# Three weight pieces issued ahead of the last batch's load in the Fourier stage, with a new order table

## The chip, the cores and the metric

The kernel runs on one core of one Trainium2 chip, as one launch. The metric is the time of a launch on the device in microseconds (us). Before the change three runs took 1112.25, 1106.89 and 1110.59 us; their median is 1110.59 us. The profiled execution, from which every duration below comes, is a fourth one: it took 1107.66 us, of which its span (first to last instruction) is 1105.9 us.

## The reference

Three blocks follow one another on inputs of batch 4, sequence 576 and width 512 (8 heads of 64):

```python
# 1. attention with a relative-position bias from a small MLP
scores = q @ k.T / 8 + bias                     # bias: relu(x * w1 + b1) @ w2, per head
x = softmax(scores) @ v                         # 4 x 8 x 576 x 64 -> x: 4 x 576 x 512
# 2. Fourier mixing, layer norm, MLP
u = x + real(fft(fft(x, axis=1), axis=2))
un = (u - mean(u)) / sqrt(var(u) + 1e-6)
x = u + relu(un @ w_ch1) @ w_ch2                # 512 -> 2048 -> 512
# 3. spatial gating
h = relu(x @ w_in)                              # 512 -> 1024, halves u and v
v_s = w_spatial @ normalize(v) + b_spatial
out = (u * v_s) @ w_out
```

## The kernel before, in words

The kernel is a sequence of phases on one core: the bias, attention, the Fourier stage, the MLP and the gating. Matrix products are done in float32 on TensorE (PE); VectorE (DVE), ScalarE (ACT) and GpSimd (POOL) prepare and evict; all loads and stores of these phases stand in one queue, SyncE's (SP).

**Attention.** A loop over `d` takes two units of 128 rows per step, 72 steps and eight more to drain (`attention_phase`). Every second pair of probability tiles is transposed by a DMA (`turn`, L483); PE reads it three steps later (`back`, L519). Finished rows go to a buffer in device memory, `xd[b]`, one per batch (`store`, L569 and L572). At the end of each step the loop calls `after(n)`, with `n = d - 72`.

**Loads for the Fourier stage.** `after` is made by `first_folds`. A batch's load (`Folds.loads`, L747) reads `xd[b]` back in six parts: 128, 128, 127, 128, 1 and 64 rows of 512 numbers (256, 256, 254, 256, 2 and 128 KB), after a step that only writes zeros. For batch 0 the steps are spread over attention: one is taken at `n = -36, -34, ...` until they are used up. Batches 1 and 2 are loaded at `n = 0` and `n = 3`. Batch 3 needs the last rows that attention stores, and is loaded in the Fourier stage.

**Fourier stage.** Per batch `b`: DVE folds the rows (`T0`, `X0`, `F00`, `F01`, then `T1`, `X1`, `F10`, `F11`; L764, L775, L782); PE makes four products `pe`, `me`, `po`, `mo` with the cosine and sine tables (L877), each into one of two PSUM banks `y`; ACT copies each out (`keep`, L881) and so frees the bank; PE makes `D` from two of them (`second`, L907, one PSUM tile for all), ACT evicts it (`d`, L914), PE transposes the rows into one of two tiles `xs` (`residual`, L895 and L897), and DVE adds the two, twice per half: `+` (L917) and `-` (L925), which frees `xs`. ACT also copies corners (L884), gathers (L888) and one crossed row (`r`, L922).

**What else runs in that stage** (`early`): the MLP's first four weight pieces and its first normalisation. A piece `w0` to `w3` (`piece`) is a DMA of 512 KB from SP into one of three staging buffers `w64` (L1695); ACT scales it (`wsq`, L1034), DVE merges it with three instructions (L1041, L1044, L1047), which frees the buffer, and ACT and DVE split it (L1703, L1706). The sums, means and squares of the first chunks (L1616 to L1677) are `n0`, `n1`, `h`, `l`, `q`, `a`, `f0`, `n2`, `c1`.

**What sets the order.** `Plan.run` builds one list out of all these operations, each with assumed durations, resources to take and give, and what it comes after. It repeatedly emits the operation with the smallest start time less its `RANK`. Each engine then executes its own operations strictly in that order: one that waits holds up all behind it on its engine. SP likewise: a DMA whose issue waits holds up all issues behind it. After the stage the MLP's first product is L1358 (`h`), whose weight pieces go on through `Weights.step` (L1072).

Of the kernel before, what the change touches and what calls it, by code (L numbers as in the profile page):

```python
# [18 lines left out]
B, H, S, D = 4, 8, 576, 64  # L19
# [624 lines left out]
def phases(tc, nc, io, vs, low, raw, xd, ident, tables, after, right):  # L644
# [28 lines left out]
W_SCALE = 2.0**-112  # L673
TP = 290
T2 = 289
F_LOAD = -36
X_LOAD = 0, 3
FOLDS = {2: 2, 3: 2, 4: 2, 5: 2}
YB = 2
AFTER = (0,)  # L680
PRINT = False
RANK = {
# [4 lines left out]
}  # L687
READY = 0.0, 2.0, 6.0, 14.0

# [103 lines left out]
def first_folds(folds):  # L793

    todo, loads = [], folds.loads(0)

    def after(n):
        if F_LOAD <= n < 0 and n % 2 == 0:
            next(loads, int)()
        if n == 0:  # L800
            folds.open()
            todo.extend(folds.steps(0))
        if n in X_LOAD:
            folds.load(1 + X_LOAD.index(n))
        for _ in range(FOLDS.get(n, 0)):
            todo.pop(0)[2]()

    return after
# [45 lines left out]
def fft_phase(tc, nc, folds, tabs, ut, bank, extra, es):  # L854
# [14 lines left out]
    def stage1(b, nm):  # L869
        F = folds.two[b % 2]  # L870
        y = ps[b, nm] = ps_y.tile([128, 512], F32, tag="y", name="y")
        z, o = dict(pe=(0, 0), me=(0, 129), po=(1, 0), mo=(1, 128))[nm]
        seq = [(128, F[z][0:r, k, o : o + 128], tt[0:r, z, k]) for k, r in rows]
        if nm == "po":
            seq[1:1] = [(1, F[0][0:r, k, 128:129], tt[0:r, 0, k]) for k, r in rows]
        for n, (m, st, mv) in enumerate(seq):
            nc.tensor.matmul(out=y[0:m, 0:TP], lhsT=st, rhs=mv, start=(n == 0), stop=(n == len(seq) - 1))  # L877

    def keep(b, nm):
        ys[b, nm] = yp.tile([128, TP], F32, tag=nm, name="y", bufs=YB)  # L880
        nc.scalar.activation(out=ys[b, nm], in_=ps.pop((b, nm))[:, 0:TP], func=AF.Copy)  # L881

    def corner(b):
        nc.scalar.activation(out=xs[b][:, :, 0:1], in_=xs[b][:, :, 256:257], func=AF.Copy)  # L884

    def gather(b, e, s):
        col = 257 + e if s else e
        nc.scalar.activation(out=folds.near[e][:, :, s], in_=xs[b][:, :, col : col + 255 : 2], func=AF.Copy)  # L888

    def residual(b, e, y):  # L890

        t = Xs[b, e, y] = ps_x.tile([128, 2, 512], F32, tag="xs", name="xs")
        for s in range(2):
            for k in (0, 1):
                nc.tensor.transpose(t[:, s, 128 * k : 128 * k + 128], folds.near[e][:, 3 * y + k, s], ident)  # L895
            i = ident[0:65, 64::-1] if y else ident[0:65, 0:65]
            nc.tensor.transpose(t[:, s, 256:321], folds.near[e][0:65, 2, s], i)  # L897

    def second(b, e):
        D = Ds[b, e] = ps_d.tile([128, 2, 512], F32, tag="D", name="D")  # L900
        for s in range(2):
            if e == 0:
                seq = [(fs[:, s], ys[b, "pe"]), (fs[:, 2 + s], ys[b, "po"])]
            else:
                seq = [(fs[:, 4], ys[b, "me"]), (fs[:, 5 + s], ys[b, "mo"])]
            for n, (st, mv) in enumerate(seq):
                nc.tensor.matmul(out=D[:, s, 0:TP], lhsT=st, rhs=mv, start=(n == 0), stop=(n == len(seq) - 1))  # L907
# [4 lines left out]
    def evict(b, e):  # L912
        d = ds[b, e] = yp.tile([128, 2, TP], F32, tag="d", name="d", bufs=2)
        ends[1] = nc.scalar.activation(out=d, in_=Ds[b, e][:, :, 0:TP], func=AF.Copy)  # L914

    def add(b, e):
        nc.vector.tensor_tensor(  # L917
            out=out(b, e)[:, :, 0:T2], in0=Xs.pop((b, e, 0))[:, :, 0:T2], in1=ds[b, e][:, :, 0:T2], op=ALU.add
        )

    def cross(b):
        nc.scalar.activation(out=ds[b, 0][0:1], in_=Ds[b, 0][0:1, ::-1, 0:TP], func=AF.Copy)  # L922

    def mirror(b, e):
        ends[0] = nc.vector.tensor_tensor(  # L925
            out=out(b, e)[:, :, T2:S], in0=Xs.pop((b, e, 1))[:, :, 287:0:-1], in1=ds.pop((b, e))[:, ::-1, 287:0:-1],
            op=ALU.add,
        )

    plan = Plan({"y": 2, "xs": 2, "D": 1, "d": 2, "F0": 1, "F1": 1, "n0": 1, "n1": 1, "w64": 3, "wsq": WSQB})  # L930
    add_op = plan.add
    for b in range(B):
        f = f"F{b % 2}"
        if b == B - 1:
            add_op("load", "load", [("SP", 0.5)], lambda: folds.load(B - 1), start=3.0)
        if b:
            last = (b - 1, "F11") if b > 1 else None
            for nm, us, go in folds.steps(b):
                add_op(
                    (b, nm), f"fold{b}", [("DVE", us)], go, after=([last] if last else []) + (["load"] if b == B - 1 else []),  # L940
                    take=[f] if nm == "F00" else [], start=READY[b],
                )
                last = b, nm
        for nm, us, need in (("pe", 1.5, "F00"), ("me", 1.5, "F01"), ("po", 3.0, "F10"), ("mo", 1.5, "F11")):
            add_op(
                (b, nm), nm, [("PE", us)], lambda b=b, nm=nm: stage1(b, nm), after=([(b, need)] if b else []) + ([(b, x) for x in ("pe", "me", "po")] if nm == "mo" else []),
                take=["y", f] if not b and nm == "pe" else ["y"],
            )
            add_op(
                (b, nm, "y"), "y", [("ACT", 0.4)], lambda b=b, nm=nm: keep(b, nm), after=[(b, nm)],  # L950
                take=[f"{nm}y"], give=["y", f] if nm == "mo" else ["y"],
            )
        add_op((b, "c"), "c", [("ACT", 0.2)], lambda b=b: corner(b), after=[(b, "X1")] if b else [])
        for e in range(2):
            k = b, e
            for s in range(2):
                add_op(
                    (k, "g", s), "g", [("ACT", 0.89)], lambda b=b, e=e, s=s: gather(b, e, s),
                    after=[(k, "g", 0)] if s else [(b, "c")], take=[] if s else [f"n{e}"],
                )  # L960
            for y in range(2):
                add_op(
                    (k, "x", y), f"x{y}", [("PE", 0.75)], lambda b=b, e=e, y=y: residual(b, e, y),
                    after=[(k, "x", 0)] if y else [(k, "g", 1)], take=["xs"], give=[f"n{e}"] if y else [],
                )
            two = ("me", "mo") if e else ("pe", "po")
            add_op(
                (k, "D"), "D", [("PE", 2.0)], lambda b=b, e=e: second(b, e), after=[(b, nm, "y") for nm in two],
                take=["D"], give=[f"{nm}y" for nm in two],
            )  # L970
            add_op((k, "d"), "d", [("ACT", 0.65)], lambda b=b, e=e: evict(b, e), after=[(k, "D")], take=["d"],
                   give=["D"] if e else [])
            add_op((k, "+"), "+", [("DVE", 0.76)], lambda b=b, e=e: add(b, e), after=[(k, "d"), (k, "x", 0)],
                   give=["xs"])
            if not e:
                add_op((k, "r"), "r", [("ACT", 0.64)], lambda b=b: cross(b), after=[(k, "+")], give=["D"])
            add_op((k, "-"), "-", [("DVE", 0.75)], lambda b=b, e=e: mirror(b, e),
                   after=[(k, "x", 1), (k, "+") if e else (k, "r")], give=["xs", "d"])
# [611 lines left out]
def tail(tc, nc, io, folds, tabs, low, right, out, es):  # L1590
# [150 lines left out]
    with ExitStack() as e1:  # L1741
        with tc.manual_schedule():
            ends = fft_phase(tc, nc, folds, tabs, ut, bank, early, e1)
# [189 lines left out]
```

## Time and profile before

| what | us |
|---|---|
| three runs | 1112.25, 1106.89, 1110.59 (median 1110.59) |
| the profiled execution | 1107.66 |
| its span | 1105.9 |
| attention ends on PE, first Fourier products | about 386 |
| PE stands still | 399.2 to 420.1 |
| first MLP product | 470.03 |
| MLP and gating | 470 to 1105.9 |

PE is busy 91% of the span, DVE 63%, ACT 49%, POOL 27%. The mean says little here, since the stages differ: from 400 to 420 us no compute engine does anything, and from 500 to 580 us PE never stops. A row of the profile names the source line, the engine, and "out<-in" by tile names; numbers in brackets are the idle time before the instruction and what ended it. `w` is the staging buffer of a weight piece, `lowb`, `raw` and `x` hold the folded batches' rows, `lowa` is the stage's output, `pt<-hl` the transposing DMA of attention.

### The profile page before, as it was taken

To read this page: it belongs to the slowest core of one execution; us is meant where nothing else is said; L and a number is where in the kernel's file an instruction comes from. 1 tells how busy PE (TensorE), PEld (TensorE's weight loads), DVE (VectorE), ACT (ScalarE), POOL (GpSimd) and SP (SyncE) were. 2 spreads that over 40 slices of the span, in tenths; PEclk is the share of its full clock that TensorE was granted. 3 is DMA by queue.
4 is the path that set the end of the run, shared out by engine and by line. 5 is a ranking of instruction groups with operands and counts; after the bars stand their busy time and mean duration, and the time that the engine had idled before them with its cause. 6 is when DMAs were issued, how large, how long until landed. Compare 5 with 4: busy or idle time off the path is not lost.

```text
span 1105.9 us, 25418 instructions
## 1 busy us (share of the span) xinstructions
PE 1010.6 (91%) x10547; PEld 924.4 (84%) x10547; DVE 692.1 (63%) x1812; ACT 546.2 (49%) x1034; POOL 293.8 (27%) x284
## 2 busy tenths in 40 slices
PE   6989888889688838999999999999999999999998
PEld 3777777778678725789999999999999989998897
DVE  5999887888678837787894342334693265262611
ACT  3888788888689514654541121211353244333322
POOL 3667786868488100000000000000002030110000
PEclk8999899999899978999999999999999999999999
DMA  5542068878978540124540000000241000101011
GB/s 175 174 128 79 14 145 165 180 168 183 158 165 164 123 134 26 39 72 139 155 133 1 1 2 1 1 1 1 78 153 55 1 1 1 39 1 48 1 39 48
DMA packets 116167, 88.22 MB, mean 80 GB/s; under 512 B 85840, under 2 KB 96340, under 8 KB 116052
## 3 DMA queue, kind: packets, MB, share of 16 engines
q1 hardware_dynamic: 113184, 79.82, 28.8%
q10 hardware_dynamic: 2724, 5.90, 1.6%
q8 instruction: 82, 1.34, 0.5%
q0 software_dynamic: 144, 0.89, 0.2%
q14 instruction: 33, 0.27, 0.1%
HBM read 57.10 MB, written 9.44 MB: 60 GB/s over the span
## 4 chain that ended last, share of the span: by engine, by line
PE 67%; DVE 13%; DMA 7%; POOL 5%; issue 4%; ACT 3%; SPq 1%; ACTq 0%; POOLq 0%; DVEq 0%
PE h L1358 18%; PE acc L1394 18%; PE psp L1530 5%; PE pu L1505 4%; PE po L1552 4%; PE pv L1453 3%; POOL hl L470 3%; PE sc L417 2%; PE po L519 2%; DMA pt<-hl 2%; DVE mask L243 2%; PE y L877 2%; DVE bt L320 2%; PE turn L493 2%; PE bps L276 2%
## 5 line engine op out<-in xcount | busy, mean ns | idle before, releaser
L1362 ACT ACTIVATE gh<-h 128x256 fp32r<-128x256 f32 x144 | 55.1, 383 | 242.4 <-PE h L1358 236.7
L1363 DVE SCALAR_TENSOR_TENSOR gl<-h,gh 128x256 fp32r<-128x256 f32 x144 | 60.7, 422 | 170.4 <-ACT gh L1362 169.9
L1358 PE MATMUL h<-uh,wh 128*128 128x256 f32 x576 | 161.5, 281 | 2.2 <-DVE gl L1363 2.0
L1394 PE MATMUL acc<-gh,wh 128*128 128x256 f32 x576 | 163.1, 283 | 0.0
L1394 PE MATMUL acc<-gh,wl 128*128 128x256 f32 x576 | 161.1, 280 | 1.4 <-DVE wl L1066 1.4
L1358 PE MATMUL h<-uh,wl 128*128 128x256 f32 x576 | 160.9, 280 | 1.0 <-DVE wl L1066 1.0
L1394 PE MATMUL acc<-gl,wh 128*128 128x256 f32 x576 | 161.0, 279 | 0.0
L1358 PE MATMUL h<-ul,wh 128*128 128x256 f32 x576 | 160.8, 279 | 0.0
L1150 POOL MEMSET w<- 64x288 f32 x2 | 0.7, 337 | 457.2 <-DVE wsq L1047 457.1
L1358 PEld LDWEIGHTS h<-uh,wh 128*128 128x128 f32 x576 | 109.0, 189 | 2.9 <-DVE gl L1363 2.4
L1394 PEld LDWEIGHTS acc<-gh,wl 128*128 128x128 f32 x576 | 108.5, 188 | 1.7 <-DVE wl L1066 1.6
L1358 PEld LDWEIGHTS h<-uh,wl 128*128 128x128 f32 x576 | 108.5, 188 | 1.2 <-DVE wl L1066 1.2
L1394 PEld LDWEIGHTS acc<-gl,wh 128*128 128x128 f32 x576 | 108.9, 189 | 0.6 <-DVE gl L1363 0.3
L1394 PEld LDWEIGHTS acc<-gh,wh 128*128 128x128 f32 x576 | 108.9, 189 | 0.4
L1358 PEld LDWEIGHTS h<-ul,wh 128*128 128x128 f32 x576 | 108.8, 189 | 0.0
L453 ACT ACTIVATE P<-s,mm 128x576 f32<-128x576 f32 x144 | 103.4, 766 | 3.9 <-DVE mm L445 3.6
L519 PE MATMUL po<-vp,pt 128*128 128x65 f16 (+3 forms) x2324 | 85.9, 198 | 8.9 <-DMA pt<-hl 7.5
L519 PEld LDWEIGHTS <-pt 128*128 128x128 f16 (+1 forms) x2324 | 82.6, 103 | 12.3 <-DMA pt<-hl 8.2
L470 POOL TENSOR_TENSOR hl<-P,hl 128x1024 f16<-128x1024 f32 x68 | 86.1, 1287 | 20.3 <-ACT hl L464 13.7
L493 PE MATMUL turn<-ident,P 128*128 128x128 f32 x380 | 58.6, 286 | 28.4 <-DVE pt L502 27.8
L276 PE MATMUL bps<-g,mask 128*128 128x64 f16 x1152 | 62.3, 195 | 16.3 <-DVE lowb L310 8.3
L493 PEld LDWEIGHTS turn<-ident,P 128*128 128x128 f32 x380 | 41.5, 143 | 41.1 <-DVE pt L502 16.6
(256 smaller groups left out, 2589.5 us busy)
## 6 DMA issues: line engine op xcount, KB each, us to landing
w<-in_w_ch SPq DMA_DIRECT2D x32, 512.0 KB
vld<-in_v ACTq DMA_DIRECT2D x16, 320.0 KB
raw<-in_q SPq DMA_DIRECT2D x16, 320.0 KB
raw<-in_v SPq DMA_DIRECT2D x16, 320.0 KB
raw<-in_k SPq DMA_DIRECT2D x16, 288.0 KB
xd<-x SPq DMA_DIRECT2D x16, 256.0 KB
w<-in_w_in SPq DMA_DIRECT2D x8, 512.0 KB
out<-o SPq DMA_DIRECT2D x16, 256.0 KB
```

The source lines that it names most:

```text
L276: nc.tensor.matmul(out=full(ps, it // 2)[:, it % 2, :, gi], lhsT=ms[gi][:, 128 * it + 64 * (it // 2) :][:, 0:128], rhs=g[:, k], start=(k = ...
L453: nc.scalar.activation(out=P[:, x, 0:S], in_=s, func=AF.Exp, bias=mm[:, 1, x : x + 1], scale=1.0)
L470: nc.gpsimd.tensor_tensor(out=hl[:, :, o : o + c], in0=P[:, :, j : j + c], in1=hl[:, :, j : j + c], op=ALU.subtract)
L493: nc.tensor.transpose(t[:, 128 * k : 128 * k + 128], P[:, 128 * k : 128 * k + 128], ident)
L519: nc.tensor.matmul(out=po[c, t % 4, 0:w], lhsT=pt[:, x, c], rhs=vp[:, j, hh, f : f + w], start=(i == 0), stop=(i == len(seq) - 1),)
L1358: nc.tensor.matmul(out=h, lhsT=st[:, q], rhs=mv[:, k], start=(n == 0), stop=(n == 11))
L1362: nc.scalar.activation(out=gh, in_=h, func=AF.Relu)
L1363: nc.vector.scalar_tensor_tensor(out=gl, in0=h, scalar=0.0, in1=gh.bitcast(F32), op0=ALU.max, op1=ALU.subtract)
L1394: nc.tensor.matmul(out=acc[x, d // 2][:, d % 2], lhsT=st[:, q], rhs=mv, start=(e == 0 and d % 2 == 0 and n == 0), stop=(e == NF - 1 and d ...
L1505: nc.tensor.matmul(out=p[:, 0:CH], lhsT=st[:, q], rhs=mv[:, kk, e], start=(n == 0), stop=(n == 11))
L1530: nc.tensor.matmul(out=p[:, 0:CH], lhsT=st, rhs=mv, start=(n == 0), stop=(n == len(seq) - 1))
L1552: nc.tensor.matmul(out=p, lhsT=st[:, f, c], rhs=mv, start=(n == 0), stop=(n == 11))
```

## The change

Three edits:

1. In the Fourier stage's list, the load of the last batch (`load`) now comes after the DMA issues of the pieces `w0`, `w1` and `w2`, and is planned with 6.0 us of SP, not 0.5. Hence in SP's queue three weight pieces stand ahead of the six parts of the load.
2. The parts of batch 0's load are taken at other steps of attention: `n = -42, -41, -37, -33, -32, -28, -24`, not `-36, -34, ..., -24`.
3. The `RANK` table has other numbers, so that the whole stage's list comes out in another order. No operation is added or removed; line numbers from L677 on grow by one, from the load's call on by two.

```diff
-F_LOAD = -36
+F_LOAD = -42
+F_STEPS = 3, 4, 8
...
 RANK = {
-    "pe": 0.9, "y": 0.7, "me": 0.9, "po": -0.5, "mo": 2.4, "c": -0.5, "g": 0.1, "x0": 0.3, "x1": 2.7, "D": 0.4,
...
+    "pe": 1.1, "y": 0.4, "me": 0.1, "po": -0.3, "mo": 3.8, "c": 0.8, "x0": 0.3, "x1": 2.6, "D": 0.4, "d": 1.1,
...
     def after(n):
-        if F_LOAD <= n < 0 and n % 2 == 0:
+        if F_LOAD <= n < 0 and n % 9 in F_STEPS:
             next(loads, int)()
...
         if b == B - 1:
-            add_op("load", "load", [("SP", 0.5)], lambda: folds.load(B - 1), start=3.0)
+            add_op("load", "load", [("SP", 6.0)], lambda: folds.load(B - 1),
+                   after=[(f"w{n}", 0) for n in range(3)], start=3.0)
```

SP at the end of attention and the start of the Fourier stage (`xd_77` is the buffer of batch 3: first attention's last stores to it, then the load from it), before:

```order
L569 DMA xd_77<-x 128x4x128
L572 DMA xd_77<-x 64x64 x2
L747 DMA lowb<-xd_77 128x512 x2
L747 DMA lowb<-xd_77 127x512
L747 DMA lowb<-xd_77 128x512
L747 DMA lowb<-xd_77 1x512
L747 DMA lowb<-xd_77 64x512
L1695 DMA w_8662<-in_w_ch 128x1024
L1695 DMA w_8684<-in_w_ch 128x1024
L1695 DMA w_8693<-in_w_ch 128x1024
L1695 DMA w_8742<-in_w_ch 128x1024
```

The same place with the change:

```order
L569 DMA xd_77<-x 128x4x128
L572 DMA xd_77<-x 64x64 x2
L1697 DMA w_8645<-in_w_ch 128x1024
L1697 DMA w_8648<-in_w_ch 128x1024
L1697 DMA w_8650<-in_w_ch 128x1024
L748 DMA lowb<-xd_77 128x512 x2
L748 DMA lowb<-xd_77 127x512
L748 DMA lowb<-xd_77 128x512
L748 DMA lowb<-xd_77 1x512
L748 DMA lowb<-xd_77 64x512
L1697 DMA w_8798<-in_w_ch 128x1024
```

The pieces `w0` to `w2` moved from behind the load to ahead of it; the fourth stays behind it.

DVE around the first fold of the last batch (`lowb_69<-lowb_69` is `T0` of batch 3, `F2571_8321` its `F00` and `F01`, the `wsq` rows are the merge of `w1`), before:

```order
L764 TENSOR_TENSOR lowb_69<-lowb_69 128x2x512
L775 TENSOR_TENSOR uv0_8317<-lowb_69 128x258
L775 TENSOR_TENSOR uv0_8317<-lowb_69 128x516
L925 TENSOR_TENSOR lowa_59<-xs_8676,d_8752 128x2x287
L917 TENSOR_TENSOR lowa_59<-xs_8765,d_8789 128x2x289
L1041 TENSOR_SCALAR wsq_8739<-wsq_8739 128x512
L1044 SCALAR_TENSOR_TENSOR wsq_8739<-w64_8684,wsq_8739 128x512
L1047 SCALAR_TENSOR_TENSOR wsq_8739<-w64_8684,wsq_8739 128x512
L925 TENSOR_TENSOR lowa_59<-xs_8799,d_8789 128x2x287
L1616 TENSOR_TENSOR w64_8818<-lowa_59 128x256
L1616 TENSOR_TENSOR w64_8818<-w64_8818,lowa_59 128x256
L782 TENSOR_TENSOR F2571_8321<-uv0_8317 128x3x129
```

The same stretch with the change:

```order
L765 TENSOR_TENSOR lowb_69<-lowb_69 128x2x512
L776 TENSOR_TENSOR uv0_8317<-lowb_69 128x258
L776 TENSOR_TENSOR uv0_8317<-lowb_69 128x516
L918 TENSOR_TENSOR lowa_59<-xs_8778,d_8776 128x2x289
L926 TENSOR_TENSOR lowa_59<-xs_8678,d_8750 128x2x287
L1043 TENSOR_SCALAR wsq_8743<-wsq_8743 128x512
L1046 SCALAR_TENSOR_TENSOR wsq_8743<-w64_8648,wsq_8743 128x512
L1049 SCALAR_TENSOR_TENSOR wsq_8743<-w64_8648,wsq_8743 128x512
L783 TENSOR_TENSOR F2571_8321<-uv0_8317 128x3x129
```

`T0` of batch 3 stands at the same place among DVE's rows; the fold `F00` behind it comes three instructions sooner: the second `-` of batch 0 and two sums of `n0` went behind the folds.

SP in attention, where batch 0 is loaded (`x_71<-xd_74` are its parts), before:

```order
L483 DMA_TRANSPOSE pt<-hl 128x18x128
L747 DMA x_71<-xd_74 128x512
L483 DMA_TRANSPOSE pt<-hl 128x18x128
L382 DMA raw<-in_k 128x576
L382 DMA raw<-in_q 128x640
L569 DMA xd_75<-x 128x4x128
L572 DMA xd_75<-x 64x64 x2
L747 DMA x_71<-xd_74 127x512
L483 DMA_TRANSPOSE pt<-hl 128x18x128
```

The same stretch with the change:

```order
L483 DMA_TRANSPOSE pt<-hl 128x18x128
L748 DMA x_71<-xd_74 127x512
L748 DMA x_71<-xd_74 128x512
L483 DMA_TRANSPOSE pt<-hl 128x18x128
L382 DMA raw<-in_k 128x576
L382 DMA raw<-in_q 128x640
L569 DMA xd_75<-x 128x4x128
L572 DMA xd_75<-x 64x64 x2
L483 DMA_TRANSPOSE pt<-hl 128x18x128
```

The 127-row part moved one transposing DMA earlier, and the fourth part came up beside it.

## Rows read from the trace of the kernel before

**Rows 1.** Busy us by stretch: PE, PEld, DVE, ACT, POOL; clock, DMA share, GB/s

```profile
400.00:420.00 20.00, 0.00 (x0) 0.00 (x0) 0.18 (x1) 0.87 (x2) 0.00 (x0) 0.52 0.43 137
...
460.00:470.00 10.00, 10.00 (x63) 8.13 (x62) 8.38 (x17) 5.56 (x11) 0.00 (x0) 1.00 0.32 105
```

**Rows 2.** Waits from 385 to 425: who, for whom; total us, times, longest

```profile
ACT wsq L1034 <- DMA w<-in_w_ch: 24.2, 1, 24.2
...
PE y L877 <- ACT y L881: 21.0, 1, 21.0
```

**Rows 3.** Chain that ended last, 385 to 425: start us, us, what

```profile
391.38 9.54 DMA xd<-x
...
402.12 4.42 SPq L747
...
407.89 11.21 DMA w<-in_w_ch
...
420.14 3.27 PE y L877 x6
```

**Rows 4.** Timeline of SP's queue, 360 to 425: start us, us issuing

```profile
391.95 2.94 SPq L572 DMA_DIRECT2D xd<-x  x2
400.94 6.86 SPq L747 DMA_DIRECT2D lowb<-xd  x6
```

**Rows 5.** DMA: issues by size; GB/s in 40 slices of 400 to 424

```profile
lowb<-xd SPq DMA_DIRECT2D x2, 254.0 KB
...
GB/s 20 1 0 116 348 372 44 14 27 24 27 34 116 328 106 256 225 396 372 375 318 328 311 161 31 24 24 27 27 20 27 27 27 27 20 7 0 0 137 328
```

**Rows 6.** Timeline of DVE, batch 3's first folds

```profile
429.51 1.22 DVE L764 TENSOR_TENSOR lowb<-lowb 128x1024 f32<-128x1024 f32 x1
430.64 1.02 DVE L775 TENSOR_TENSOR uv<-lowb 128x258 f32<-128x258 f32 x2
431.59 0.75 DVE L925 TENSOR_TENSOR lowa<-xs,d 128x574 f32<-128x574 f32 x1
...
432.94 0.42 DVE L1041 TENSOR_SCALAR wsq<-wsq 128x512 int32<-128x512 int32 x1
433.40 0.69 DVE L1044 SCALAR_TENSOR_TENSOR wsq<-w,wsq 128x512 int32<-128x512 int32 x1
...
436.83 1.02 DVE L782 TENSOR_TENSOR F<-uv 128x387 f32<-128x387 f32 x2
```

**Rows 7.** Timeline of PE, 415 to 475: start us, us, operation

```profile
436.69 2.12 PE L907 MATMUL D<-y,fs 128*128 128x290 f32 x8
438.65 3.10 PE L877 MATMUL y<-tt,F 128*128 128x290 f32 x12
...
446.53 4.91 PE L877 MATMUL y<-tt,F 128*128 128x290 f32 x18
...
470.03 0.36 PE L1358 MATMUL h<-uh,wh 128*128 128x256 f32 x1
```

**Rows 8.** Timeline of SP's queue in attention, 235 to 320

```profile
265.63 0.80 SPq L747 DMA_DIRECT2D x<-xd  x1
267.19 3.23 SPq L483 DMA_TRANSPOSE pt<-hl  x1
...
273.25 0.51 SPq L747 DMA_DIRECT2D x<-xd  x1
274.44 11.62 SPq L483 DMA_TRANSPOSE pt<-hl  x1
```

**Rows 9.** Timeline of PE in attention, 255 to 300

```profile
274.41 1.02 PE L519 MATMUL po<-vp,pt 128*128 128x65 f16 x28
...
288.09 2.70 PE L519 MATMUL po<-vp,pt 128*64 128x65 f16 x56 [7.12 <-DMA pt<-hl]
```

**Rows 10.** Busy us by stretch, columns as in Rows 1: the clock

```profile
424.00:425.00 1.00, 1.00 (x4) 0.66 (x4) 0.90 (x3) 0.97 (x3) 0.00 (x0) 0.68 0.60 246
...
300.00:310.00 10.00, 8.90 (x149) 8.00 (x149) 9.11 (x25) 9.05 (x13) 6.30 (x7) 1.00 0.78 128
```

6 rows, old and new, of the table RANK are left out of this document.

## The prediction

> **What bounds the kernel now.** I read first the busy times by stretch, because the page's mean of 91% for PE hides where it is lost. From 400 to 420 us all compute engines stand still, while ten microseconds before the MLP PE is busy 10.00 of 10 [rows 1]. So the Fourier stage has one hole, and behind it PE is the bound. The waits of the hole come next: ACT waits 24.2 us for a weight piece, and PE 21.0 us for ACT's copy `y` [rows 2]. ACT needs nothing of that piece for the Fourier products; the scaling of `w0` merely stands ahead of the copy in ACT's order, and PE has no free bank. Why the piece is late, the chain in order of time tells: attention's last store to `xd[3]` lands 9.54 us after its issue, at 400.92; only then SP issues the last load, whose third part alone holds the queue 4.42 us; `w0` is issued behind it at 407.89 and lands 11.21 us later, at 419.10; PE resumes at 420.14 [rows 3]. The load's issues take 6.86 us in all, and the stores before it were issued by 394.89 [rows 4]. SP thus stands idle from 394.89 to 400.94, waiting for the store.
>
> Last I asked why 512 KB took 11.21 us. In the rates of 400 to 424 the traffic falls from over 300 GB/s to 20 to 31 GB/s and stays there from 414.4 to about 420.4 [rows 5]. I read this as one of the 16 DMA engines working on alone: 400 GB/s, about the highest rate in that row, over 16 is 25. A load's third part has 127 rows and 254 KB [rows 5]; if one engine moves it all, that takes 254 KB / 25.5 = 10 us (an estimate from the tail's rate), and what is queued behind it on that engine waits, the sixteenth share of each weight piece too.
>
> The Trainium skill says the same outright (DMA: Bandwidth & Descriptors, Why a DMA increments its semaphore by 16 and not by 1): a transfer uses the largest number of engines up to 16 that divides its slowest dimension, and 127 partitions come down to one. The tail agrees with that. By the page's 27 GiB/s per engine the part would take some 9 us, and every end below of the load would come about 1 us sooner.
>
> **The change part by part.** *The pieces ahead of the load.* `w0` can be issued at about 395, as soon as SP is through the stores. Its share on the slow engine (512/16 = 32 KB, 1.3 us at 25 GB/s) stands behind the store that lands at 400.92 [rows 3], so `w0` lands at about 402.2, and if all three shares are worked on together, at 404.8. I take 402.4. ACT scales it and PE resumes a microsecond later, as 420.14 follows 419.10 [rows 3]: 403.4, so 16.7 us earlier. That is the most this edit can give.
>
> *The load behind them.* Its first part still waits for the store, hence is issued at 400.94 as now, but on the slow engine three shares of 32 KB now go first (3.8 us). The load's own bytes there are 16 + 16 + 254 + 16 + 8 = 310 KB, or 12.2 us at 25.5 GB/s. End: 400.9 + 3.8 + 12.2 = 416.9. In the trace that engine moved 342 KB (load and `w0`) from 401.5 to 419.1, 19.4 GB/s on average with the other pieces beside it; at this rate all 406 KB end at 421.8. Little else moves in the new 406 to 417, so I lean to the first and take 418.0. `w3`, behind the load, lands at about 419.5; ACT meets it between two copies.
>
> *The new wait.* DVE's order has `T0` of batch 3, and that needs the load. With the copies resuming at 403, DVE gets through batch 2's folds and reaches `T0` at about 412, so it now waits some 6 us at its head, with everything behind it. Before, it ran there at 429.51 with no wait [rows 6]. What hides this is PE's own backlog. From its restart to `D` of batch 1 PE worked 436.69 - 420.14 = 16.5 us [rows 3, 7]; from 403.4 that ends at 419.9. It then needs the `-` that stands two adds behind `T0`. In DVE's rows `T0` to `X0` takes 1.13 us, `X0` to the add 0.95, the two adds 1.35, the merge 1.9 (0.42 + 0.69 + 0.69 and gaps) [rows 6]. So the `-` ends at 418.0 + 3.4 = 421.5: PE waits 1.6 us, makes an `xs` and `D` (0.6 + 2.0) until 424.1. `F00` of batch 3 begins at 418.0 + 5.3 = 423.3 and is done at 423.9, in time: in the old order the third add and two sums stood in between and it began 7.3 us behind `T0` [rows 6]. PE starts batch 3's products at 424.1 and not at 438.65 [rows 7]: 14.5 us earlier.
>
> *What the new order gives back.* The add and the sums that moved now come after all of batch 3's folds, and that add frees an `xs`. Walking the rows on with the same durations, PE waits about 1.3 us for it, so that batch 2's `po` begins at 433.3 where it began at 446.53 [rows 7]: -13.2. The reciprocal root of the first chunk falls behind batch 3's products and DVE's last adds slip 0.4: the MLP's first product comes at 457.2 instead of 470.03, **-12.8 us**. Of the remaining RANK moves I count nothing: PE had no gap above 0.2 us from there to 470 (10.00 of 10, [rows 1]) and hides them; without that cover a displaced DVE or ACT operation costs its 0.4 to 1.5 us. The MLP's later pieces are issued as far ahead of its first product as before, so the gain is kept to the end.
>
> *Batch 0's parts.* In attention the 127-row part is issued at 273.25; the transposing DMA next in SP's queue is issued at 274.44, is held 11.62 us [rows 8], and PE waits 7.12 us for it, until 288.09 [rows 9], that is 14.8 us behind the part. Now the part goes where a small one stood at 265.63, with the next transpose at 267.19 [rows 8]; its reader on PE is the product at 274.41 [rows 9]. At the same 14.8 us, with 0.7 more for the fourth part beside it, it lands at 280.4 to 281.1: a stall of 6.0 to 6.7 us, against 7.12. I take **-0.4 us**, with ends of -7.1 (no stall) and +3 (the queue behind it late too). The other parts only change places.
>
> *Sum.* -12.8 - 0.4 = -13.2 us. On the profiled execution's 1107.66 us that is 1094.5; it lies 2.9 below the median of the three runs, 1110.59, on which it is 1097.4. I predict **1097 us**.
>
> **The rivals.** *(A) The wait moves instead of going.* The load or `w3` lands some 6 to 8 us later than I have it, because three pieces and the load share the slow engine worse than by my rates, or because SP is held at the 127-row part for 11.62 us, as behind such a part in attention [rows 8], rather than 4.42 [rows 3]. From 416.4 on each microsecond of `T0` is one of the end; `T0` at 425 leaves 12.8 - 7 = 5.8 and about 1104. Against it: the tail of rows 5 is steady, and the engine has to move the 310 KB anyway while SP is held. At `T0` = 431 nothing would be left.
>
> *(B) Slower: the clock.* After the hole TensorE is granted 1.2 GHz, a mean of 0.52 there [rows 1], and is back at 2.4 GHz only from about 424.6, after 4.5 us of work (mean 0.68 in that microsecond, [rows 10]). If the new stage, with short waits at 421, 428 and 433, were run at 1.2 GHz to its end, PE's work, 470.03 - 420.14 [rows 7] less 2.3 lost at the low clock, 47.6 us, would take twice that: 403.4 + 95.2 = 498.6, 28.6 us late, 1139. The change ends slower once over 26 us are run at the low clock. Against: in attention PE had waits of up to 2 us and kept 2.4 GHz (1.00 at 8.90 busy of 10, [rows 10]).
>
> *(C) Attention gives back.* Both the transpose at 267.19 and the next one are held, and PE stalls twice: +7, about 1104. For it: the parts are no smaller. Against: the next issue is 7 us further on.
>
> *(D) The change doesn't do what it says:* `w0` is not issued at 395 but held until the store has landed. It then lands at 404.8 at the latest, still well ahead of the load, which sets the end: 1097 again.
>
> **How the numbers follow.** The forecast with (D) 0.77, (A) 0.13, (C) 0.06, (B) 0.04. The forecast's own range is 1092 to 1102: the load's end at 416.9 or 421.8 is -1.1 or +3.8, the attention term -3 or +2, and the base is either of two 2.9 apart. Eight times in ten needs a part of (A) and (C) too: 1091.5 to 1106. This kernel's runs spread so that about 0.5%, 5.6 us, can be told from no change: faster means under 1105.0. The forecast, half of (A) and most of (C) lie there: 0.84. The rest of (A) and a gain eaten in attention: same 0.11. Slower 0.05.
>
> **What would show it.** Right: ACT's wait for `w` falls from 24.2 to about 7 us; PE's hole ends near 403; DVE has a wait of about 6 us on the load ahead of `T0` of batch 3, at 418; PE starts batch 3's first product at 424 and the MLP at 457; a PE wait of 6 to 7 us on `pt` stands near 274. Wrong: a DVE wait on the load until 425 or later, ACT held by `w3` with PE idle behind it, a low clock through the stage, or an MLP whose first pieces are late by what was won.

## The result and the profile after

The changed kernel takes 1096.45 us in the median of four runs (1091.44 to 1098.06), the kernel before 1110.63 (1106.89 to 1112.25): a ratio of 0.9869, 95% interval 0.9828 to 0.9911. It is 14 us faster; 1097 us, within 1091.5 to 1106, was forecast. The profiled execution of the changed kernel took 1098.06 us, with a span of 1096.3.

The hole of the Fourier stage is nearly gone. The busy times by stretch of the changed kernel, columns as in [rows 1]:

```profile
400.00:420.00 20.00, 16.50 (x57) 10.72 (x57) 9.39 (x15) 7.41 (x15) 0.00 (x0) 0.83 0.46 156
420.00:440.00 20.00, 18.67 (x90) 12.79 (x89) 18.49 (x36) 10.64 (x21) 0.00 (x0) 1.00 0.01 3
440.00:460.00 20.00, 20.00 (x114) 15.35 (x113) 15.16 (x30) 12.95 (x24) 0.00 (x0) 1.00 0.18 53
```

PE works 16.50 of the 20 us in which it did nothing before [rows 1], and from 420 on the granted clock is 1.00, that is 2.4 GHz. In the kernel before it was 0.88 from 420 to 440:

```profile
420.00:440.00 20.00, 19.86 (x78) 14.29 (x79) 18.92 (x32) 10.88 (x22) 0.00 (x0) 0.88 0.09 29
```

The waits of the changed kernel from 385 to 430, which answer to [rows 2]:

```profile
DVE lowb L765 <- DMA lowb<-xd: 9.2, 2, 4.8
...
ACT wsq L1036 <- DMA w<-in_w_ch: 7.8, 2, 7.6
...
PE y L878 <- ACT y L882: 3.5, 1, 3.5
```

ACT's wait for the first weight piece fell from 24.2 us to 7.6, PE's for ACT's copy from 21.0 to 3.5. DVE now waits twice for a load, which it did not before: 4.75 us for batch 2's (its `T0` stood behind the merge of `w0` before and stands ahead of it now) and 4.43 us for the last one. SP's queue and the chain of the changed kernel show what held what, as [rows 3, 4] did. First the queue:

```profile
383.57 10.48 SPq L748 DMA_DIRECT2D lowb<-xd  x6
394.14 0.53 SPq L569 DMA_DIRECT2D xd<-x  x1
394.72 2.99 SPq L572 DMA_DIRECT2D xd<-x  x2
397.82 5.41 SPq L1697 DMA_DIRECT2D w<-in_w_ch  x3
404.02 7.94 SPq L748 DMA_DIRECT2D lowb<-xd  x6
```

Then the chain that ended last, 385 to 430:

```profile
394.14 9.86 DMA xd<-x
...
405.20 15.74 DMA lowb<-xd
```

The three pieces are issued from 397.82, ahead of the load, but it takes 5.41 us until all three are out. For most of that SP waits. Its own waits in the same stretch have:

```profile
SPq L1697 <- DMA lowb<-xd: 4.1, 2, 3.9
```

The second piece reads nothing of batch 2's load, for which SP waits 3.9 us here. In the packed trace it counts its landing on the semaphore that the 127-row part of that load uses, and it is issued as soon as that part has landed, at 402.3. The store still needs 9.86 us to land. What `T0` of batch 3 waits for last, landing 15.74 us after its issue at 405.20, is the load's fourth part (128 rows), issued right behind the 127-row one. On DVE and PE (timeline) this gives:

```profile
403.00 1.23 DVE L765 TENSOR_TENSOR lowb<-lowb 128x1024 f32<-128x1024 f32 x1 [4.75 <-DMA lowb<-xd]
...
421.13 1.22 DVE L765 TENSOR_TENSOR lowb<-lowb 128x1024 f32<-128x1024 f32 x1 [4.43 <-DMA lowb<-xd]
```

```profile
388.30 3.19 PE L878 MATMUL y<-tt,F 128*128 128x290 f32 x12
...
406.38 3.27 PE L878 MATMUL y<-tt,F 128*128 128x290 f32 x6 [3.50 <-ACT y L882]
...
426.95 1.74 PE L878 MATMUL y<-tt,F 128*128 128x290 f32 x6
...
435.59 4.91 PE L878 MATMUL y<-tt,F 128*128 128x290 f32 x18
...
459.08 0.36 PE L1360 MATMUL h<-uh,wh 128*128 128x256 f32 x1
```

In the attention the 127-row part is issued at 266.48, and the transpose behind it is held 9.22 us instead of 11.62 [rows 8]; PE waits 6.31 us, where it waited 7.12 [rows 9], and 0.28 us once more. SP and PE of the changed kernel there:

```profile
266.48 3.80 SPq L748 DMA_DIRECT2D x<-xd  x2
270.45 9.22 SPq L483 DMA_TRANSPOSE pt<-hl  x1
```

```profile
269.97 1.03 PE L519 MATMUL po<-vp,pt 128*128 128x65 f16 x28 [0.28 <-DMA pt<-hl]
...
281.76 1.71 PE L519 MATMUL po<-vp,pt 128*128 128x65 f16 x28 [6.31 <-DMA pt<-hl]
```

### The profile page after: what moved, and what is told of

Same layout as the page of the kernel before. It is cut to its first block, busy times and chain, and to the rows that moved or that the text cites. A ratio compares the mean times of both kernels' runs of the same rounds, so it can differ in the third digit from the quotient of the medians.

```text
span 1096.3 us, 25413 instructions
## 1 busy us (share of the span) xinstructions
PE 1017.9 (93%) x10547; PEld 928.3 (85%) x10547; DVE 692.5 (63%) x1812; ACT 546.2 (50%) x1034; POOL 293.6 (27%) x284
## 4 chain that ended last, share of the span: by engine, by line
PE 65%; DVE 14%; POOL 8%; issue 5%; DMA 4%; ACT 3%; SPq 1%; ACTq 0%; POOLq 0%; DVEq 0%
PE h L1360 18%; PE acc L1396 18%; PE psp L1532 5%; PE pu L1507 4%; PE po L1554 4%; POOL hl L470 4%; PE pv L1455 3%; DVE mask L243 2%; PE po L519 2%; DVE bt L320 2%; PE turn L493 2%; PE bps L276 2%; PE sc L417 2%; DMA lowb<-xd 1%; DVE pt L502 1%
```

## The experiments

Twelve kernels ran. Those sent together share a chip and the runs of the kernel before; ratios are to that kernel, with 95% intervals. The marker for "how late the tail starts" is PE's first product `acc` of the MLP (475.61 us before, 464.67 after): unlike `h`, which some orders start early, it has the same work behind it in all of them.

**Which part of the change brings the gain.** Three kernels with one part each, and one with two.

`order_alone`: the kernel before, and

```
-            add_op("load", "load", [("SP", 0.5)], lambda: folds.load(B - 1), start=3.0)
+            add_op("load", "load", [("SP", 6.0)], lambda: folds.load(B - 1),
+                   after=[(f"w{n}", 0) for n in range(3)], start=3.0)
```

> The kernel before with one edit: the last batch's load stands behind the first three weight pieces in SyncE's order; ranks and the first batch's load steps are the old ones. Theory (the wait of the weight piece behind the load is the whole loss): w0 is issued about 10 us earlier, ScalarE waits about 7 us for it instead of 24, TensorE starts again near 404 to 406 us, and the kernel takes 1096 to 1100 us against 1110.6. Rival (the new ranks carry the gain, by another order on ScalarE or TensorE): 1104 us or more.

Measured: 1100.98 us, ratio 0.9923 (0.9899 to 0.9946), a microsecond above the theory's range. ACT's wait fell to 8.7 us and PE restarted at 405.42, as the theory has it. But then PE lost time that the changed kernel doesn't lose. Its waits in `order_alone`, 385 to 470:

```profile
PE y L877 <- ACT y L881: 5.5, 1, 5.5
PE xs L895 <- DVE lowa L925: 2.5, 2, 2.0
PE xs L895 <- DVE lowa L917: 2.0, 3, 1.2
```

With the old ranks PE waits 4.5 us in all for DVE's adds, in the changed kernel 1.2. The longest of these waits, 1.97 us until 448.64, is for a `-` that stands on DVE behind the reciprocal root of the first chunk (`f0`), for which DVE itself has to wait for ACT; the new ranks put that root later. DVE there, and the busy times of the stretch, columns as in [rows 1]:

```profile
446.16 0.42 DVE L995 TENSOR_TENSOR w<-rs,w 128x256 f32<-128x256 f32 x1 [1.85 <-ACT rs L993]
```

```profile
440.00:460.00 20.00, 17.34 (x84) 12.29 (x82) 10.96 (x22) 10.82 (x20) 0.00 (x0) 0.91 0.08 26
```

PE is busy 17.34 us here and 20.00 in the changed kernel. The granted clock is 0.91 against 1.00: behind the wait of 1.97 us PE worked at 1.2 GHz from 449 to about 452. So such a wait costs more than its own length.

`rank_alone`: the kernel before with the new table `RANK` and nothing else.

> The kernel before with the new ranks alone; the load still stands ahead of all weight pieces. Theory (the weight piece is late because of the load ahead of it): the hole of TensorE at 399 to 420 us stays within 4 us of its 20.9 us, and the time is 1107 to 1111 us. Rival (the ranks put the copies that TensorE waits for ahead of the scaling on ScalarE): the hole shrinks by over 8 us and the time is below 1103 us.

Measured: 1118.93 us, ratio 1.0072 (1.0049 to 1.0095). Neither: the hole stayed, as the theory said, and the time came out 9 us worse. PE's waits in it from 385 to 484, then its stretches:

```profile
PE y L877 <- ACT y L881: 19.9, 1, 19.9
PE xs L895 <- DVE lowa L917: 2.2, 2, 1.3
```

```profile
420.00:440.00 20.00, 17.55 (x77) 12.68 (x78) 17.58 (x31) 10.96 (x21) 0.00 (x0) 0.88 0.11 31
440.00:460.00 20.00, 17.01 (x67) 10.78 (x65) 14.52 (x32) 10.80 (x24) 0.00 (x0) 0.91 0.01 1
```

Behind the hole PE works 34.56 of 40 us; in the kernel before 39.86 (19.86 and 20.00). The first `acc` comes 8.3 us later than there, at 483.88. The clock fell again here, to 0.91 from 440 to 460. My reading is that the ranks order the stage for a load that lands late and pieces that land early, and so cost 9 us where the pieces are the late ones; no run takes single ranks apart.

`steps_alone`: the kernel before with `F_LOAD = -42` and `n % 9 in F_STEPS`.

> The kernel before with one edit: the first batch's six parts are issued on other steps of the attention. Theory: the 127-row part meets another transpose, the wait of TensorE for it is 6.0 to 6.7 us instead of 7.1, the time 1110.2 us (1109.5 to 1111). Rival (the new steps are what made the attention of the changed kernel 2 us longer): 1112 to 1113 us, with the 2 us already there at the Fourier stage's first product.

Measured: 1109.17 us in 12 runs, ratio 0.9992 (0.9978 to 1.0007). The sign fits -0.4 us, but the interval holds zero (the time itself lies 0.3 us below the range, on a base of 1109.9). The rival's +2 us is outside it.

`order_rank`: both other parts, with the old steps.

> The kernel before with the load behind three weight pieces and the new ranks, but the old load steps in the attention. Theory (the ranks only pay with the new order: alone the order brought 8.9 us, the ranks alone cost 9.0, the steps alone brought 0.7): the two together carry all but the steps' part, 1096 to 1098 us on a base of 1110. Rival (the steps do more than alone once the rest is changed): over 1099 us.

Measured: 1096.29 us, ratio 0.9866 (0.9845 to 0.9887), the changed kernel's gain without the steps. So order and ranks are one change: -8.9 and +9.0 us alone, -14.7 together.

**What holds the store and the pieces: 127 rows on one DMA engine.**

`after_split`: the changed kernel, and

```
-        for p, k, lo, n in (0, 0, 0, 128), (0, 1, 128, 128), (1, 3, 256, 127), (0, 4, 383, 128), (64, 2, 511, 1), (0, 2, 512, 64):
+        for p, k, lo, n in (0, 0, 0, 128), (0, 1, 128, 128), (1, 3, 256, 112), (113, 3, 368, 15), (0, 4, 383, 128), (64, 2, 511, 1), (0, 2, 512, 64):
```

> The changed kernel with the 127-row part of each batch's load issued as two, 112 rows and 15 rows. Theory (127 rows go through a single DMA engine, at 25 GB/s, and hold the queue's next transpose and the Fourier stage's fold T0 of batch 3): the transpose held 9.2 us in the attention takes about 4 us, TensorE's wait there falls from 6.6 us to 0 to 2 us, the last batch's load lands 4 to 7 us earlier and batch 3's first product comes 1 to 3 us earlier; 1088 to 1092 us. Rival (the load is held by the queue's order or by the store ahead of it, not by the one engine): 1095 to 1097 us, the last part landing no earlier.

Measured: 1080.47 us, ratio 0.9727 (0.9694 to 0.9759), 16 us better than the changed kernel and about twice the most that the theory gave. SP's queue in the attention and ahead of the Fourier stage:

```profile
265.97 1.11 SPq L748 DMA_DIRECT2D x<-xd  x2
267.27 3.19 SPq L483 DMA_TRANSPOSE pt<-hl  x1
...
383.66 1.47 SPq L1697 DMA_DIRECT2D w<-in_w_ch  x3
385.22 3.83 SPq L748 DMA_DIRECT2D lowb<-xd  x7
```

Hardly anything holds SP any more: 1.47 us for the three pieces instead of 5.41, 3.83 for the last load instead of 7.94, and the transpose is held 3.19 us instead of 9.22. The rates tell why. GB/s in 40 slices of the same length (0.6 us), of the changed kernel from 400 to 424 and of the split from 380 to 404:

```profile
GB/s 416 102 24 24 24 151 92 410 417 416 382 300 389 130 27 24 27 24 34 174 273 171 256 256 382 89 24 24 24 27 24 24 24 27 24 27 20 0 0 14
```

```profile
GB/s 0 0 0 0 44 346 74 27 75 321 382 410 416 403 403 386 396 410 352 283 328 222 294 369 14 0 0 0 0 0 27 0 0 0 0 0 0 0 0 0
```

The runs of 24 to 27 GB/s, a sixteenth of the 417 GB/s at the peak, I read as one engine working on alone; in the split kernel they are gone, and the load and the four pieces pass in one block of some 10 us. PE has no wait for ACT left in the stage, and works 20.00 of 20 us from 400 to 420 and from 420 to 440.

Three kernels split the part for one batch only (`if b == 0`, `2` or `B - 1`, else 127 rows).

> The changed kernel with the 127-row part split into 112 and 15 rows for batch 0 alone, whose parts are issued in the attention. Theory: the transpose behind it is no longer held 9.2 us, TensorE's wait of 6.6 us there goes and nothing takes its place; 1089 to 1091 us, the Fourier stage as long as in the changed kernel. Rival (ScalarE and the turns of the block behind it are late by as much): over 1094 us.

Measured: 1088.16 us, ratio 0.9805 (0.9779 to 0.9831), 0.8 us below the range. PE's wait on `pt` fell from 6.6 us (6.31 and 0.28) to 0.3, and nothing took its place:

```profile
PE po L519 <- DMA pt<-hl: 0.3, 1, 0.3
```

The stage behind, from its first product to the first `acc`, took 76.05 us (378.86 to 454.91), as in the changed kernel (76.37).

> The changed kernel with the 127-row part split for batch 2 alone, whose load is issued just ahead of the last batch's store. Theory (the store, and with it the weight pieces and the last load, wait behind batch 2's 127 rows on one DMA engine): the store lands 4 to 6 us earlier after its issue than the 9.9 us of the changed kernel, the weight pieces' issue takes 1.5 us instead of 5.4, the first weight piece lands before ScalarE needs it and TensorE's hole of 3.5 us goes; 1090 to 1093 us. Rival (the store itself takes its time): no earlier landing, 1096 us.

Measured: 1089.36 us, ratio 0.9800 (0.9774 to 0.9826), 0.6 us below the range. SP's queue in it:

```profile
390.59 0.38 SPq L569 DMA_DIRECT2D xd<-x  x1
391.02 1.16 SPq L572 DMA_DIRECT2D xd<-x  x2
392.29 1.47 SPq L1698 DMA_DIRECT2D w<-in_w_ch  x3
393.86 9.02 SPq L748 DMA_DIRECT2D lowb<-xd  x6
```

The load, which must wait for the store, is issued 3.3 us after the store instead of 9.9. So the store was slow because batch 2's 127 rows, just ahead of it in the queue, were still on their engine. The packed trace of the kernel before, which marks the landing on each engine, has it directly: of the store's sixteen engines fifteen are through by 394.19 and one at 400.92, and batch 2's 127-row part, which has a single engine, lands at 399.16. ACT's wait for `w` is down to 0.2 us, and PE's hole of 3.5 us is gone.

> The changed kernel with the 127-row part split into 112 and 15 rows for the last batch alone, whose load is issued in the Fourier stage. Theory: only what follows that load is won: its last part lands about 5 us earlier, fold T0 of batch 3 and batch 3's first product come 1 to 3 us earlier; 1093 to 1095 us, the attention and the restart of TensorE as in the changed kernel. Rival (the last load carries most of the 16 us that the split of all four brought): below 1089 us.

Measured: 1091.87 us, ratio 0.9828 (0.9811 to 0.9845), a microsecond below the theory's range. Batch 3's `T0` runs at 414.40 with no wait (421.13 in the changed kernel), while PE's hole stays, at 4.8 us.

```profile
414.40 1.22 DVE L766 TENSOR_TENSOR lowb<-lowb 128x1024 f32<-128x1024 f32 x1
```

By the ratios the splits for batch 0, 2 and 3 are worth about 7, 8 and 4.5 us over the changed kernel, together more than the 16 of all four batches: the shares overlap, and batch 1's was not taken alone.

`before_split`: the kernel before with the same split, and no part of the change.

> The kernel before with nothing but the 127-row part of each batch's load issued as 112 and 15 rows. Theory (the one DMA engine that takes 127 rows holds up what stands behind it in SyncE's queue: the transposes of the attention, the last batch's store and the first weight piece): the attention ends 7 to 10 us earlier, the store ahead of the last load lands 4 to 5 us after its issue instead of 9.5, and TensorE's hole of 20.9 us falls to 8 to 14 us; 1090 to 1098 us. Rival (only the load's order makes the hole): the hole stays at 17 us or more, and only the attention's part is won, 1100 to 1104 us.

Measured: 1081.95 us, ratio 0.9736 (0.9721 to 0.9752), well below both ranges: theory and rival gave the one engine too little. Its chain, 380 to 400, and the one wait for ACT that PE has left:

```profile
383.56 2.21 DMA xd<-x
...
388.98 5.51 DMA w<-in_w_ch
...
394.51 0.66 ACT wsq L1034
```

```profile
PE y L877 <- ACT y L881: 1.6, 1, 1.6
```

The store lands in 2.21 us instead of 9.54 [rows 3]; the first piece, still issued behind the whole load, in 5.51 instead of 11.21 [rows 3]. PE's hole falls from 21.0 us to 1.6 with the order untouched, where 8 to 14 were expected. Beside it, the changed kernel with the split (0.9727) is no better than the intervals allow to tell: once the part is split, the change is worth nothing that could be measured.

**Is it the one engine?** Three more forms of the same part in the changed kernel. `after_126` has `(1, 3, 256, 126), (127, 3, 382, 1)`; `after_113` has `(1, 3, 256, 113), (114, 3, 369, 14)`; `after_double` has two 127-row parts:

```
-        for p, k, lo, n in (0, 0, 0, 128), (0, 1, 128, 128), (1, 3, 256, 127), (0, 4, 383, 128), (64, 2, 511, 1), (0, 2, 512, 64):
+        for p, k, lo, n in (0, 0, 0, 128), (0, 1, 128, 127), (127, 1, 255, 1), (1, 3, 256, 127), (0, 4, 383, 128), (64, 2, 511, 1), (0, 2, 512, 64):
```

> The changed kernel with the 127-row part of every batch as 126 rows and 1 row. Theory (the rows go in equal shares to the largest number of DMA engines, up to 16, that divides their count: 126 = 14 x 9 goes to 14, 127 is prime and goes to one): like the split into 112 and 15 rows, 1079 to 1084 us, the transpose beside the load in the attention 3 to 4 us. Rival (any part that isn't a multiple of 16 rows goes to one engine): 1094 to 1097 us.

Measured: 1080.25 us, ratio 0.9728 (0.9702 to 0.9755): as good as 112 and 15.

> The changed kernel with the 127-row part as 113 rows and 14 rows. Theory (113 is prime, so its 226 KB go through one DMA engine as the 254 KB did, 1.1 us less per load): 1091 to 1096 us, a transpose held 8 to 9 us in the attention. Rival (the number of parts, or that the part is shorter, is what the split into 112 and 15 rows gained by): 1080 to 1084 us.

Measured: 1094.10 us, ratio 0.9864 (0.9828 to 0.9900): nothing won. It has as many parts as the two fast forms, and a shorter long one; what counts is how the number of rows divides. The landing marks in the packed traces agree: a part of 127 or 113 rows has two, one at its issue and one when it lands, as with one engine; one of 126 rows has fifteen and one of 112 rows sixteen.

> The changed kernel with the suspected cost doubled: the 128-row part ahead of the 127-row one is issued as 127 rows and 1 row, so that each batch has two parts of 254 KB on one DMA engine. Theory: if both fall to the same engine, each load lands 8 to 10 us later, the attention's wait of 6.6 us and the Fourier stage's wait for the last load grow by as much, 1108 to 1125 us; if they fall to two engines, the growth is small, 1096 to 1101 us. Rival (the one engine plays no part, 1 row more is 1 DMA more): 1096 to 1098 us with the holds on SyncE unchanged.

Measured: 1133.92 us, ratio 1.0219 (1.0190 to 1.0249), some 37 us above the changed kernel and above the theory's range. SP's queue of `after_113` in the attention, that of `after_double` at the Fourier stage, and the stretch from 406 to 414 of the latter, columns as in [rows 1]:

```profile
269.25 3.93 SPq L748 DMA_DIRECT2D x<-xd  x2
273.36 8.66 SPq L483 DMA_TRANSPOSE pt<-hl  x1
```

```profile
377.67 16.32 SPq L748 DMA_DIRECT2D raw<-xd  x7
...
397.85 19.61 SPq L748 DMA_DIRECT2D lowb<-xd  x7
417.57 0.54 SPq L569 DMA_DIRECT2D xd<-x  x1
418.15 2.88 SPq L572 DMA_DIRECT2D xd<-x  x2
```

```profile
406.00:414.00 8.00, 7.09 (x20) 4.53 (x19) 4.67 (x8) 0.53 (x2) 0.00 (x0) 0.59 0.07 25
```

For these 8 us, with both parts of batch 2's load outstanding, the DMAs move 25 GB/s, the rate of one engine and not of two. The two parts landed one behind the other, at 414.79 and 425.81 by the packed trace: both went to the same engine. With two of them in the queue SP itself stands 16 to 20 us in the issue of a load, and the last store starts at 417.57 instead of 394.14: 23.4 of the 33.5 us by which the first `acc` is later (498.18 against 464.67). The theory had counted the later landing of each load and not that SP is held by the loads of batches 1 and 2 in turn.

The Trainium skill (DMA: Bandwidth & Descriptors, Why a DMA increments its semaphore by 16 and not by 1) says that a transfer uses the largest number of engines up to 16 that divides its slowest dimension. These runs agree with it: 126 and 112 rows fast, 127 and 113 slow.

## Why the prediction was right, and where it stopped short

All events of the stage lie some 2 us later in the profiled execution than I put them, because the stage itself begins later: PE's first product is at 388.30, and in the kernel before

```profile
386.26 3.19 PE L877 MATMUL y<-tt,F 128*128 128x290 f32 x12
```

Taking these 2.04 us off, step by step:

| event | before | predicted | after | after less 2.04 |
|---|---|---|---|---|
| PE resumes | 420.14 | 403.4 | 406.38 | 404.34 |
| `T0` of batch 3 on DVE | 429.51 | 418.0 | 421.13 | 419.09 |
| PE, first product of batch 3 | 438.65 | 424.1 | 426.95 | 424.91 |
| PE, `po` of batch 2 | 446.53 | 433.3 | 435.59 | 433.55 |
| PE, first MLP product | 470.03 | 457.2 | 459.08 | 457.04 |

The stage from its first product to the MLP became 12.99 us shorter (83.77 to 70.78); the term was -12.8.

*The pieces ahead of the load.* Right: the first piece is on ACT 1.4 us behind the store's landing (405.36 against 404.00), which fits its share on the slow engine, 1.3 us. My restart was 0.9 us early, because the store landed 1.0 us later than at 400.92 (404.00 less 2.04).

*The load behind them.* The faster of my two rates was the nearer: `T0` came 1.1 us later than 418.0 with the shift taken off, 1.0 of which is the store's lateness, and is far from rival (A)'s 425. One row I read wrongly: the 4.42 us of [rows 3] are not the issue of the 127-row part, the third of six, but of the 128-row part behind it; nothing in the sum hung on it.

*The new wait.* It is there, 4.43 us against some 6, because DVE came to `T0` at 414.7 (with the shift taken off) and not at 412. PE's backlog hid it: PE waits 1.2 us for DVE's adds, where I had 1.6 and 1.3.

*What the new order gives back.* The walk held to a quarter of a microsecond at `po` and the MLP. That it is so close is partly luck: PE restarted 0.9 us later than I had it and then waited 1.7 us less for DVE's adds, and the two errors all but cancel. I had counted order and ranks as one edit by walking the new rows; the runs show that the order alone brings 8.9 us and the ranks alone cost 9.0.

*Batch 0's parts.* The stall is 6.31 and 0.28 us (6.0 to 6.7 forecast) against 7.12, -0.5 for -0.4. Rival (C), a second long stall, did not come.

*The 2 us of shift.* They are not the steps' doing as far as these runs can tell. With the old steps the first product of the stage lay at 386.26, 387.05, 386.95 and 388.58 in four profiled executions, with the new ones at 388.30, 389.89, 387.81, 390.64 and, with batch 2's part split, 386.44: the two groups overlap, and the interval of `steps_alone` leaves at most 0.8 us for the steps. What makes the shift stays open. The tail from the first `acc` to the end of the span likewise took from 629.0 to 634.4 us in the profiled executions (630.3 before, 631.6 after), which is where the other 1.3 us of the profiled difference went; no line of the profile was found for it. The medians, 14.2 us apart, come nearer to the sum of 13.2 than the two profiled spans, 9.6 apart.

*Rival (B)* fell: the clock was 1.00 from 420 to 460. Its mechanism shows for some 3 us each in `order_alone` and `rank_alone`, near 450. *Rival (D)* did not happen as written: the pieces were issued before the store had landed at 404.00, `w0` at 397.82. But `w1` and `w2` were held to 402.3 and 402.9 by the landing of batch 2's load, which the prediction did not see.

Where the working stopped short is its reading of the hole, in its first two paragraphs. It found the one engine and charged it to the last load, but took the store's 9.54 us as given. They had the same cause, one batch earlier, and `after_split_b2` shows it. So the load's place in the queue made the hole only together with the 127-row parts: `order_alone` takes it from 21.0 us to 5.5 with the parts as they are, `before_split` to 1.6 with that place unchanged. The forecast's number did not depend on this, since the change left the cause where it was.

## What to carry to other kernels

Look in the profile for stretches in which the DMA rate sits at a sixteenth of its peak (here 24 to 27 of 417 GB/s), and at the row counts of the transfers issued there: a part of 127 rows is better issued as 126 and 1 or 112 and 15. A long landing of an innocent transfer (a store, a weight piece, a transpose) should be traced to what stands ahead of it in its queue before the queue is reordered around it. Ranks that were worked out for one order are part of that order, and are to be moved and measured with it.

## What the runs showed of the hardware that was not expected

A transfer on one engine costs the issuing engine too, in two ways. An issue behind it can itself be held: of the 7.94 us for the last load of the changed kernel, 5.53 are the issue of the 128-row part behind the 127-row one, while with the part split no issue of that load took longer than 0.47; with two such parts in each load a single issue took 9.75 us, and seven DMAs 19.61. And SP can wait for its landing, as in the 5.41 us for three weight pieces, where 1.2 are issue and 3.9 are the wait for batch 2's load. Two 127-row parts with different rows and partitions fell to the same engine (landings 11 us apart, at 25 GB/s). And the small piece left over costs next to nothing: 126 rows and 1 row were as fast as 112 and 15.
